# Turning an expert's gathered rows by transposing DMA transfers instead of on TensorE

## The chip, the cores and the metric

The kernel runs on one core of a Trainium2 chip. The metric is device time in microseconds. The kernel before takes 346.95 us, the median of three runs (346.88 to 347.78). The profile shown below is of one further execution under the hardware profiler, whose span is 321.0 us; positions in it ("at 159.71") are microseconds from the start of that span.

## The reference

A linear attention with a normalisation is followed by a layer of eight experts, of which each token uses one. Cut to what matters:

```python
# q, k, v: (8 batches, 8 heads, 576 tokens, 64)
kv  = einsum('bhsd,bhse->bhde', k, v)
out = einsum('bhsd,bhde->bhse', q, kv)
out = out / sqrt(mean(out * out, -1) + 1e-6) * g_norm
x   = out.transpose(0, 2, 1, 3).reshape(4608, 512)          # one row for each token

logits     = x @ w_gate                                     # (4608, 8)
expert_idx = argmax(logits, 1)
gate_w     = softmax(logits)[token, expert_idx]
for e in range(8):                                          # w1[e]: (512, 1024), w2[e]: (1024, 512)
    mask = expert_idx == e
    y[mask] = gate_w[mask] * (maximum(x[mask] @ w1[e], 0) @ w2[e])
```

## The kernel before

The attention stage computes the normalised rows in float16 and scatters each row, with its token number and its gate weight behind it, into a scratch in DRAM that has a region for each expert. The experts' stage works through nine jobs: experts 0 to 6, one tile of left-over rows, and expert 7. An expert's job gathers up to 640 rows, five tiles of 128 rows by 512 values. The first matrix product needs the rows turned, with the 512 values on the partitions. `flip` does that, a tile at a time:

```python
def flip(self, t):
    nt, xe = self.nt, self.xe
    if t == 0:
        self.xt = PF.tile([128, 4, nt * 128], F16, tag=f"xt{nt}", bufs=2, name="xt")
        self.idx = PF.tile([128, nt], I32, tag=f"idx{nt}", bufs=3, name="idx")
    xp = PSF.tile([128, 4, 128], F16, tag="xp", bufs=2, name="xp")        # PSUM
    for c in range(4):
        nc.tensor.transpose(xp[:, c, :], xe[t][:, c * 128:(c + 1) * 128], ident16)
    nc.vector.tensor_copy(self.xt[:, :, t * 128:(t + 1) * 128], xp)
    nc.vector.scalar_tensor_tensor(out=self.idx[:, t:t + 1], ...)         # rows of the output
```

The two products, `one` for a half of the columns and a block of 128 of the 1024 hidden values, `two` for a tile of rows:

```python
def one(self, ws, f):
    hp = PSF.tile([128, wd], F32, tag="hp", bufs=3, name="hp")            # wd = 320
    for kk in range(4):
        nc.tensor.matmul(hp, self.w.w1[:, kk, f * 128:(f + 1) * 128],
                         self.xt[:, kk, ws * wd:(ws + 1) * wd], start=(kk == 0), stop=(kk == 3))
    nc.scalar.activation(self.ht[:, f, ws * wd:(ws + 1) * wd], hp, ACTF.Relu)

def two(self, t):
    yp = PSF.tile([128, D], F32, tag="yp", bufs=3, name="yp")
    for f in range(8):
        nc.tensor.matmul(yp, self.ht[:, f, t * 128:(t + 1) * 128], self.w.w2[:, f, :],
                         start=(f == 0), stop=(f == 7))
    ys = PF.tile([128, D], F32, tag="ys", bufs=4, name="ys")
    nc.vector.tensor_scalar(ys, yp, self.xe[t][:, 514:516].bitcast(F32), None, op0=ALU.mult)
    nc.gpsimd.indirect_dma_start(out=self.views[t], ... in_=ys, ...)      # scatter to the output
```

The weights of an expert come in three steps: `stage` loads w1 in float32 into a single buffer `wst` from the queue of SyncE (SP), `scale` multiplies it by the norm's gain into a float16 buffer `w1e` (three buffers), and `second` loads w2 and casts it on the way, from the queue of GpSimd. Every engine works through its instructions in the order in which this code gives them:

```python
rows(0); W[1].second(); rows(1); W[2].second()       # rows(n): the five gathers of job n, on GpSimd
zp = PSF.tile([128, 512], F32, tag="yp", bufs=3, name="yp")
zeros(zp, 8)                                         # matmuls of zeros, to keep TensorE's clock up
for t in range(CT):                                  # CT = 5
    jobs[0].flip(t)
    zeros(zp, 2)

for n in range(len(order)):                          # nine jobs
    job = jobs[n]
    # ... n == 4: the left-over tile's gather, with its own row of the table
    nxt = jobs[n + 1] if n + 1 < len(order) else None
    rows(n + 2)
    flips = list(range(nxt.nt)) if nxt is not None else []
    for ws in range(job.halves):                     # two halves
        for f in range(8):
            job.one(ws, f)
            if ws == job.halves - 1 and f >= 2 and flips:
                nxt.flip(flips.pop(0))
            if ws == (n == 0) and f % 2 == 1 and n + 2 < len(order):
                W[n + 2].scale(nc.vector, f // 2)
                if f == 7 and n + 3 < len(order):
                    W[n + 3].stage()
    for t in range(job.nt):
        job.two(t)
    if n + 3 < len(order):
        W[n + 3].second()
```

Of the kernel before, what the change touches and what calls it, by code (L numbers as in the profile page):

```python
# [11 lines left out]
F32 = mybir.dt.float32  # L12
F16 = mybir.dt.float16
I32 = mybir.dt.int32
ALU = mybir.AluOpType
ACTF = mybir.ActivationFunctionType
AXX = mybir.AxisListType.X
# [4 lines left out]
def _bc(ap: bass.AP, insert_pos: int, count: int) -> bass.AP:  # L22
    dims = [list(d) for d in ap.ap]
    dims.insert(insert_pos, [0, count])
    return bass.AP(tensor=ap.tensor, offset=ap.offset, ap=dims)
# [3 lines left out]
def kernel(  # L29
# [11 lines left out]
    nc = tc.nc  # L41
# [3 lines left out]
    D = H * Dh  # L45
# [10 lines left out]
            name=f"I-{nc.next_id()}", act_func_set_id=ACT_SET_LN_EXP, ins=[], outs=[]  # L56
        )
    )

    xs = nc.dram_tensor("xs_scratch", (E * N, RW // 2), I32, kind="Internal")  # L60
    xs_views = dram_disjoint_views(xs.ap(), N // 128)
# [40 lines left out]
    ident16 = ch[:, 0:128]  # L102
# [10 lines left out]
    rowf = P_const.tile([128, E, CT], F32, tag="rowf")  # L113
    rowi = P_const.tile([128, E, CT], I32, tag="rowi")
    tabb = P_const.tile([128, 32], F32, tag="tabb")
# [6 lines left out]
    def zeros(t, n):  # L122

        for _ in range(n):
            nc.tensor.matmul(t, zero16, _bc(zero16, 1, 4), start=True, stop=True)
# [34 lines left out]
    with (  # L160
# [5 lines left out]
        for n in range(4):  # L166
            t = PA.tile([128, 4, 144], F32, tag=f"kvs{n}", name=f"kvs{n}")
# [252 lines left out]
        for b in range(1, B):  # L420
            f = first_slot[b]
# [137 lines left out]
    with (  # L559
# [14 lines left out]
        class Job:  # L574
# [8 lines left out]
            def flip(self, t):  # L583

                nt, xe = self.nt, self.xe
                if t == 0:
                    self.xt = PF.tile(
                        [128, 4, nt * 128], F16, tag=f"xt{nt}", bufs=2, name="xt"
                    )
                    self.idx = PF.tile([128, nt], I32, tag=f"idx{nt}", bufs=3, name="idx")  # L590
                xp = PSF.tile([128, 4, 128], F16, tag="xp", bufs=2, name="xp")
                for c in range(4):
                    nc.tensor.transpose(  # L593
                        xp[:, c, :], xe[t][:, c * 128:(c + 1) * 128], ident16
                    )
                nc.vector.tensor_copy(self.xt[:, :, t * 128:(t + 1) * 128], xp)  # L596

                nc.vector.scalar_tensor_tensor(
                    out=self.idx[:, t:t + 1], in0=xe[t][:, 512:514].bitcast(I32),
                    scalar=self.okm[:, t:t + 1], in1=self.bgm[:, t:t + 1],  # L600
                    op0=ALU.mult, op1=ALU.add,
                )
# [58 lines left out]
        with tc.manual_schedule(engines=by_hand):  # L661
            jobs = []
            for n, e in enumerate(order):
                if e == "left":
                    jobs.append(None)
                    continue
                jobs.append(Job(
                    [xe_bufs[(n % 3) * CT + t] for t in range(CT)], W[n],
                    valid[:, e, :], bigm[:, e, :], out_views[e * CT:(e + 1) * CT],
                ))  # L670

            def rows(n):
                if n < len(order) and order[n] != "left":
                    for t in range(CT):
                        gather(jobs[n].xe[t], rowi[:, order[n], t:t + 1])

            rows(0)
            W[1].second()
            rows(1)
            W[2].second()  # L680
            zp = PSF.tile([128, 512], F32, tag="yp", bufs=3, name="yp")
            zeros(zp, 8)
            for t in range(CT):
                jobs[0].flip(t)
                zeros(zp, 2)

            for n in range(len(order)):
                job = jobs[n]
                if n == 4:
                    jobs[7] = left_over(0, 3 * CT, out_views[E * CT])  # L690
                    W[7] = jobs[7].w
                nxt = jobs[n + 1] if n + 1 < len(order) else None
                rows(n + 2)
                flips = list(range(nxt.nt)) if nxt is not None else []
                for ws in range(job.halves):
                    for f in range(8):
                        job.one(ws, f)
                        if ws == job.halves - 1 and f >= 2 and flips:
                            nxt.flip(flips.pop(0))
                        if ws == (n == 0) and f % 2 == 1 and n + 2 < len(order):  # L700
                            W[n + 2].scale(nc.vector, f // 2)
                            if f == 7 and n + 3 < len(order):
# [6 lines that stand above are left out]
        nov = nc.values_load(tabi[0:1, 1, 7:8], min_val=0, max_val=NOV)  # L709
        with tc.If(nov > 1):  # L710
            with tc.For_i(1, nov) as t:
                job = left_over(t, 3 * CT, out_views[E * CT + 1])
# [36 lines left out]
```

## Time and profile before

| what | value |
|---|---|
| time, median of three | 346.95 us |
| span of the profiled execution | 321.0 us |
| TensorE busy | 276.2 us (86%) |
| VectorE busy | 161.1 us (50%) |
| ScalarE busy | 125.3 us (39%) |
| GpSimd busy | 160.8 us (50%) |
| transposes of gathered rows on TensorE (L593) | 164, mean 225 ns |
| copies of turned tiles on VectorE (L596) | 41, mean 419 ns |
| a w1 load (`wst`), from issue to landing | 12.7 us, median of 9 |
| a w2 load (`w2e`) | 13.6 us, median of 9 |
| a gather of a tile (`xe`) | 8.6 us, median of 40 |
| a scatter of a tile to the output | 3.9 us, median of 41 |

In the profile PE is TensorE, DVE VectorE, ACT ScalarE, POOL GpSimd and SP SyncE; PEld is the loading of TensorE's stationary operand, which overlaps its matmuls. A line in order of time has start, length, engine, source line, operation, what is written and what is read, shapes and how many; in brackets stands the idle time before it and what ended that. The lengths of matmuls overlap where they are pipelined, so what one costs is read from the starts. The DMA share is the mean busy share of the 16 DMA engines; it can go a little over 1, as it adds up packets that overlap. The clock is what TensorE was granted, 1.00 being full speed.

### The profile page before, as it was taken

How to read it: one execution, taken by the hardware profiler on the slowest of the kernel's cores; microseconds unless marked ns; L12 is line 12 of the kernel's file. 1: busy time of each engine (PE TensorE's matmuls, PEld its weight loads, DVE VectorE, ACT ScalarE, POOL GpSimd, SP SyncE). 2: the span in 40 equal slices, each digit the busy share in tenths (PEclk: the TensorE clock that was granted, in tenths of full speed). 3: DMA queues.
4: the chain of work that ended last, by engine and by line, in shares of the span. 5: the costliest groups of instructions: out<-in, count | busy, mean ns of one | idle time of the engine just before them, and what ended most of it. 6: DMA issues, size and time to landing. Idle time of an engine off the chain costs nothing.

```text
span 321.0 us, 6063 instructions
## 1 busy us (share of the span) xinstructions
PE 276.2 (86%) x2333; PEld 194.3 (61%) x2333; DVE 161.1 (50%) x415; ACT 125.3 (39%) x299; POOL 160.8 (50%) x188
## 2 busy tenths in 40 slices
PE   8769999899799397624699999999998999999990
PEld 3468978787687386511465655747465574747640
DVE  0023657857865637787426364636436273525040
ACT  1023654665465326452071532607153160713700
POOL 2095022283276626744787564836737444474041
PEclk9967999999999879857699999999999999999996
DMA  6999999999999994227699899695999969593021
GB/s 235 265 284 348 263 325 346 225 309 354 242 347 282 350 310 129 99 82 236 163 202 274 309 213 376 115 349 186 302 277 163 364 150 297 209 236 123 4 101 55
DMA packets 59726, 76.22 MB, mean 237 GB/s; under 512 B 16429, under 2 KB 50478, under 8 KB 59696
## 3 DMA queue, kind: packets, MB, share of 16 engines
q1 hardware_dynamic: 43360, 47.42, 48.6%
q0 software_dynamic: 16336, 28.40, 35.7%
q8 instruction: 19, 0.31, 0.4%
q14 instruction: 11, 0.09, 0.1%
HBM read 71.70 MB, written 15.50 MB: 272 GB/s over the span
## 4 chain that ended last, share of the span: by engine, by line
DMA 30%; PE 23%; issue 16%; POOL 12%; DVE 9%; SPq 3%; ACT 2%; POOLq 1%; DVEq 0%
DMA out_dram<-ys,idx 10%; PE op L294 7%; DMA xe<-xs_scratch,rowi 6%; DMA ld<-in_v_dram 6%; POOL out_dram L634 5%; DMA w2e<-in_moe_w_dram 5%; POOL xe L565 5%; PE kvp L232 4%; PE yp L626 3%; PE qtp L276 2%; PE kgp L254 2%; PE hp L612 2%; SPq L182 2%; DMA xs_scratch<-xg,sli 2%; DVE xg L327 2%
## 5 line engine op out<-in xcount | busy, mean ns | idle before, releaser
L619 ACT ACTIVATE ht<-hp 128x320 f16<-128x320 f32 (+1 forms) x136 | 58.1, 428 | 99.9 <-PE hp L612 90.8
L612 PE MATMUL hp<-xt,w1e 128*128 128x320 f16 (+1 forms) x544 | 78.7, 294 | 0.0
L626 PE MATMUL yp<-w2e,ht 128*128 128x512 f16 x328 | 72.3, 379 | 0.0
L634 POOL DMA_INDIRECT out_dram<-ys,idx x41 | 41.6, 1015 | 60.1 <-DVE ys L631 40.7
L631 DVE TENSOR_SCALAR ys<-yp,xe 128x512 f32<-128x512 f32 x41 | 30.8, 750 | 71.6 <-PE yp L626 49.0
L612 PEld LDWEIGHTS <-w1e 128*128 128x128 f16 x544 | 50.9, 98 | 18.6
L626 PEld LDWEIGHTS <-ht 128*128 128x128 f16 x328 | 32.1, 98 | 37.2
L404 POOL DMA_INDIRECT xs_scratch<-xg,sli x36 | 34.9, 970 | 30.6 <-DVE sli L400 20.1
L565 POOL DMA_INDIRECT xe<-xs_scratch,rowi x40 | 41.7, 1043 | 15.6 <-issue 11.6
L294 PE MATMUL op<-kvs,qts 128*128 128x144 f32 (+1 forms) x320 | 47.4, 309 | 1.7 <-ACT ex L376 0.7
L294 PEld LDWEIGHTS op<-kvs,qts 128*128 128x128 f32 (+1 forms) x320 | 39.7, 190 | 4.6 <-ACT sq L310 0.9
L213 POOL COPY qp<-ld 128x512 f32<-128x512 f32 x32 | 18.4, 615 | 45.1 <-DMA ld<-in_q_dram 45.1
L315 DVE TENSOR_REDUCE ms<-sq 128x8 f32<-128x512 f32 x36 | 24.5, 680 | 16.8 <-ACT sq L310 16.7
L310 ACT ACTIVATE sq<-op 128x512 f32<-128x512 f32 x36 | 21.4, 595 | 27.6 <-PE op L294 26.9
L281 ACT COPY qts<-qtp 128x512 f32<-128x512 f32 x36 | 20.9, 581 | 21.7 <-PE qtp L276 21.7
L232 PE MATMUL kvp<-ld 128*64 128x64 f32 x512 | 23.6, 239 | 4.8 <-DMA ld<-in_v_dram 4.8
L596 DVE COPY xt<-xp 128x512 f16<-128x512 f16 x41 | 17.2, 419 | 15.9 <-PE xp L593 15.6
L232 PEld LDWEIGHTS kvp<-ld 128*64 128x64 f32 x512 | 19.0, 147 | 9.4 <-issue 8.0
L327 DVE TENSOR_TENSOR xg<-op,rinv 128x512 f16<-128x512 f32 x36 | 24.5, 680 | 0.3
L593 PE MATMUL xp<-ch,xe 128*128 128x128 f16 x164 | 16.5, 225 | 8.8 <-DMA xe<-xs_scratch,rowi 7.4
L276 PE MATMUL qtp<-cf,qp 128*128 128x128 f32 x128 | 21.2, 293 | 1.7 <-POOL qp L213 1.7
L144 DVE TENSOR_SCALAR w1e<-wst,g 128x1024 f16<-128x1024 f32 x28 | 21.1, 804 | 1.8 <-DMA wst<-in_moe_w_dram 1.8
(93 smaller groups left out, 221.4 us busy)
## 6 DMA issues: line engine op xcount, KB each, us to landing
wst<-in_moe_w_dram SPq DMA_DIRECT2D x9, 2048.0 KB, 12.7
w2e<-in_moe_w_dram POOLq DMA_DIRECT2D x9, 1024.0 KB, 13.6
ld<-in_k_dram SPq DMA_DIRECT2D x8, 1024.0 KB, 10.8
ld<-in_v_dram SPq DMA_DIRECT2D x8, 1024.0 KB, 10.7
ld<-in_q_dram SPq DMA_DIRECT2D x8, 1024.0 KB, 9.0
kr<-in_k_dram SPq DMA_DIRECT2D x8, 128.0 KB, 9.9
vr<-in_v_dram SPq DMA_DIRECT2D x8, 128.0 KB, 7.1
qr<-in_q_dram SPq DMA_DIRECT2D x8, 128.0 KB, 6.7
```

The costliest lines, as they stand in the source:

```text
L232: nc.tensor.matmul(kvp[64 * hh:64 * hh + 64, i, :], lhs, rhs, start=(j == 0), stop=(j == 4),)
L276: nc.tensor.transpose(qtp[:, i, :], src[:, 2 * i:2 * i + 2, :], ident)
L294: nc.tensor.matmul(op[c, i // 2, c0:c0 + 144], qts[s][:, i, c], kvs[:, i, :], start=True, stop=True,)
L315: nc.vector.reduce_sum(ms, sq, axis=AXX)
L327: nc.vector.tensor_tensor(xg[:, r, 0:512].rearrange("p (c i h n) -> p c i h n", c=2, i=2, h=2), ox, _bc(r4, 4, 64), op=ALU.mult,)
L404: nc.gpsimd.indirect_dma_start(out=xs_views[9 * self.P + self.g0 + t], out_offset=IndirectOffsetOnAxis(ap=self.sli[:, t:t + 1], axis=0), i ...
L565: nc.gpsimd.indirect_dma_start(out=xe.bitcast(I32), out_offset=None, in_=xs.ap(), in_offset=IndirectOffsetOnAxis(ap=rows, axis=0), bounds_ ...
L612: nc.tensor.matmul(hp, self.w.w1[:, kk, f * 128:(f + 1) * 128], self.xt[:, kk, ws * wd:(ws + 1) * wd], start=(kk == 0), stop=(kk == 3),)
L619: nc.scalar.activation(self.ht[:, f, ws * wd:(ws + 1) * wd], hp, ACTF.Relu)
L626: nc.tensor.matmul(yp, self.ht[:, f, t * 128:(t + 1) * 128], self.w.w2[:, f, :], start=(f == 0), stop=(f == 7),)
L631: nc.vector.tensor_scalar(ys, yp, self.xe[t][:, 514:516].bitcast(F32), None, op0=ALU.mult)
L634: nc.gpsimd.indirect_dma_start(out=self.views[t], out_offset=IndirectOffsetOnAxis(ap=self.idx[:, t:t + 1], axis=0), in_=ys, in_offset=None ...
```

## The change

The transposes on TensorE, the PSUM tile and the copy go; in their place SyncE's queue issues one transposing DMA transfer for each gathered tile, from SBUF to SBUF. This takes work off TensorE and VectorE. `xt` gets a third buffer, since the transfers of the next job are asked for at the beginning of a job and no longer between its matmuls. The zero matmuls around the first job's transposes are replaced by 24 matmuls on a tile of zeros that VectorE clears after it has computed the first job's row numbers.

```diff
                     self.xt = PF.tile(
-                        [128, 4, nt * 128], F16, tag=f"xt{nt}", bufs=2, name="xt"
+                        [128, 4, nt * 128], F16, tag=f"xt{nt}", bufs=3, name="xt"
                     )
 ...
-                xp = PSF.tile([128, 4, 128], F16, tag="xp", bufs=2, name="xp")
-                for c in range(4):
-                    nc.tensor.transpose(
-                        xp[:, c, :], xe[t][:, c * 128:(c + 1) * 128], ident16
-                    )
-                nc.vector.tensor_copy(self.xt[:, :, t * 128:(t + 1) * 128], xp)
+                nc.sync.dma_start_transpose(
+                    out=self.xt[:, :, t * 128:(t + 1) * 128], in_=xe[t][:, 0:D]
+                )
 ...
             zp = PSF.tile([128, 512], F32, tag="yp", bufs=3, name="yp")
-            zeros(zp, 8)
             for t in range(CT):
                 jobs[0].flip(t)
-                zeros(zp, 2)
+            late0 = PF.tile([128, 128], F16, tag="late0", name="late0")
+            nc.vector.memset(late0, 0.0)
+            for _ in range(24):
+                nc.tensor.matmul(zp, late0, _bc(late0, 1, 4), start=True, stop=True)
 ...
                 rows(n + 2)
-                flips = list(range(nxt.nt)) if nxt is not None else []
+                for t in range(nxt.nt if nxt is not None else 0):
+                    nxt.flip(t)
                 for ws in range(job.halves):
                     for f in range(8):
                         job.one(ws, f)
-                        if ws == job.halves - 1 and f >= 2 and flips:
-                            nxt.flip(flips.pop(0))
```

More of the change, by code (lines that the diff above doesn't have):

```diff
@@ L14 @@
 I32 = mybir.dt.int32
+I16 = mybir.dt.int16
 ALU = mybir.AluOpType
```

## The prediction

> **What bounds the kernel now.** I read the page first for the slices, then the instructions in order of time on TensorE, then busy time by stretch, one stretch for each expert, and last the groups and the chain of waits. In the slices
>
> ```profile
> PE   8769999899799397624699999999998999999990
> PEclk9967999999999879857699999999999999999996
> DMA  6999999999999994227699899695999969593021
> ```
>
> the first half of the span is the attention stage, which the change doesn't touch. Slices 17 to 20 (some 136 to 160 us) are the hand-over: TensorE has little to do and its clock is down to 5 to 8 tenths. From slice 20 on come the experts, with TensorE at 9 tenths and full clock to the end. Each slice is 8.0 us. Is that 9 real work, or waiting that looks like work? The order of time on TensorE answers, here for the third expert:
>
> ```profile
> 197.56 6.14 PE L612 MATMUL hp<-xt,w1e 128*128 128x320 f16 x44
> 203.53 0.39 PE L593 MATMUL xp<-ch,xe 128*128 128x128 f16 x4
> 203.76 0.71 PE L612 MATMUL hp<-xt,w1e 128*128 128x320 f16 x4
> 204.30 0.39 PE L593 MATMUL xp<-ch,xe 128*128 128x128 f16 x4
> ...
> 206.82 0.71 PE L612 MATMUL hp<-xt,w1e 128*128 128x320 f16 x4
> 207.37 8.80 PE L626 MATMUL yp<-w2e,ht 128*128 128x512 f16 x40
> 216.00 6.14 PE L612 MATMUL hp<-xt,w1e 128*128 128x320 f16 x44
> ```
>
> No idle time is printed anywhere, so TensorE sets the pace. The step from start to start is the cost (the durations overlap): 44 hp take 203.53 - 197.56 = 5.97, or 0.136 us each; 40 yp take 8.63, or 0.216 each; four transposes take 203.76 - 203.53 = 0.23. An expert is 64 x 0.136 + 40 x 0.216 = 17.3 us of matmuls, plus five turned tiles at 0.23 = 1.13, which gives the measured 18.44.
>
> The stretches, one expert each, with PE, PEld, DVE, ACT, POOL busy time, then clock, DMA share and rate:
>
> ```profile
> 178.70:197.60 18.90, 18.61 (x126) 11.30 (x125) 9.20 (x19) 7.00 (x16) 11.13 (x12) 1.00 0.97 284
> 197.60:216.00 18.40, 18.40 (x126) 11.26 (x124) 9.52 (x19) 7.00 (x16) 9.82 (x10) 1.00 0.86 247
> 234.40:254.20 19.80, 18.69 (x126) 11.34 (x125) 9.63 (x22) 7.00 (x16) 11.14 (x11) 1.00 0.94 262
> 295.00:312.40 17.40, 17.40 (x105) 10.08 (x103) 3.75 (x5) 6.99 (x16) 4.51 (x5) 1.00 0.13 47
> ```
>
> The last expert, which has no next one to turn, takes 17.4. DMA is at 0.86 to 0.97 while weights flow: the second engine close to its limit, and the one that the change loads. In the attention stage, where TensorE does wait for loads, the same column stands at 1.10 with 306 GB/s (20 to 90 us), so I take 1.1 as full.
>
> The hand-over, TensorE and GpSimd in order of time:
>
> ```profile
> 144.58 3.42 PE L125 MATMUL yp<-zero 128*128 128x512 f16 x8 [0.26 <-DVE cnt L509]
> 155.04 0.61 PE L593 MATMUL xp<-ch,xe 128*128 128x128 f16 x4 [7.04 <-DMA xe<-xs_scratch,rowi]
> 155.44 1.06 PE L125 MATMUL yp<-zero 128*128 128x512 f16 x2
> ...
> 159.71 6.14 PE L612 MATMUL hp<-xt,w1e 128*128 128x320 f16 x44
> ```
>
> ```profile
> 150.28 1.05 POOL L565 DMA_INDIRECT xe<-xs_scratch,rowi  x1 [3.71 <-DVE cm L542]
> 155.56 1.00 POOL L565 DMA_INDIRECT xe<-xs_scratch,rowi  x1 [0.31 <-issue]
> ```
>
> The first gather of the first expert lands 4.7 us after its issue, at 155.0; the fifth, issued at 155.56, 2.7 later, at 158.3. The first real matmul starts at 159.71, 1.4 us after the last row is there. TensorE turns tiles and multiplies zeros from 155.04, and the granted clock is 0.50 from 152 to 157 and 1.00 from 158: it comes up after some 2.9 us of work.
>
> **What the Trainium skill says.** "Advanced Engine Details and Errata", section "X-Bar Transpose (TRN2)", holds transposing DMAs to be as fast as ordinary ones, 350 to 400 GB/s. "DMA: Bandwidth & Descriptors", section "Latency and other measured facts", has 261 GB/s where the middle dimension isn't contiguous, as in xt here. Neither is shown by the trace of before, which has no such transfer. The same page, section "Issuing engines are not separate DMA queues", says that all queues run on the same 16 engines; the trace agrees, in that a gather lands in 2.7 us in the quiet hand-over but in 12.9 us when issued at 223.46 behind w2e and beside wst. "TensorE: Matmul & The Clock Gate", section "Part 4: PE-mode transpose", gives about 275 ns for a transpose in a kernel; the mean recorded here is 225 ns, but back to back one costs only 0.23 / 4 = 57 ns of TensorE's time, and that is what removing it saves.
>
> **The change, part by part.**
>
> 1. Transposes off TensorE. Inside the experts' stage 36 tiles are turned (experts 1 to 7 have five each, the left-over tile one; those of expert 0 lie before it): 36 x 0.226 = -8.1 us, all on the path.
>
> 2. Copies off VectorE: 41 copies of 0.419 us are 17.2 us, no bound by themselves. But VectorE works in order, and where it waited for an output scatter (ys waiting for out_dram, 15.7 us in four waits) the copy came late and TensorE stopped. From 159.71 to 312.35 is 152.6 us; the matmuls need 8 x 17.3 + 3.5 for the left-over tile = 141.9, the transposes 8.1, so 2.6 us are such stops (the longest are 1.11, 0.34 and 0.29, with the matmuls around them stretched). The new feed of xt doesn't pass VectorE: -2.6.
>
> 3. The hand-over. SP now waits for each gather, transposes it, and TensorE waits. The W[2] load issued on SP at 146.38 lands in 8.3 us, at 154.7, so it isn't in the way. What is in the way is the block of 24 warming matmuls: they read late0, which VectorE clears only after the fifth idx, and that waits for the fifth gather at 158.3. Add some 0.4 for idx and memset: start at 158.7, with a cold clock, since the zeros between 144 and 159 are gone. At 0.43 us each (3.42 / 8) the first 2.9 us hold seven; the other 17 at 0.216 take 3.7. They end at 165.3. The three tiles that the first half needs have gathers landed by 156.0, and even at 2 us each would be turned by 163. So the first hp starts at about 165.4 instead of 159.71: +5.7.
>
> 4. Load on DMA. A tile is 128 x 512 x 2 bytes = 131 KB, at 261 GB/s 0.5 us of all engines, an estimate from the page above. Five per expert are 2.5 us. Now an expert's DMA work is about 0.9 x 18.5 = 16.7 in units of the share; with 2.5 it is 19.2, and at 1.1 it fits in 17.4 us, just as long as an expert will take (17.3). There is slack of most of an expert between a weight's landing and its use, and xt has three buffers, so a shortage comes out only in part. I put +2.6 for it, half a microsecond for each of the five experts during which weights still come.
>
> Sum: -8.1 - 2.6 + 5.7 + 2.6 = -2.4 us, 346.95 - 2.4 = 344.5. I carry the difference from the profiled span (321.0) to the unprofiled time one to one.
>
> **Rivals.** (a) The transposes are hidden and DMA has room: the term of 2.6 is nothing, and the time is 341.9. For it: each is asked for nearly an expert ahead, and only 0.13 of DMA is used in the last expert. Against: the 0.97 above. (b) DMA becomes the bound. The wst buffer is single: load (12.7 us median), four scalings on VectorE (3.0), next load, a loop of 15.7, and the transposes go through the same queue. Up to about 1.5 us for the five they fit into 17.3; at 2 us per tile the loop is 25.7, a drift of 8 per expert over five loops, less some 6 us before VectorE's wait reaches yp. That would make 360 to 375. For it: in the chain of waits DMA holds 30% and PE 23%, and GpSimd's round of w2e, five gathers and five scatters already takes 18.5 us (222.2 to 240.67), waiting 4.4 us for landings. Against: the skill's rates are four times better than 2 us. (c) The hand-over is worse than I have it, as expert 0's transposes take 3 us each beside the gathers of expert 1: first hp at 168 or later, 347 to 350. The writer's choice of 24 warming matmuls hints that they expected a wait of that length.
>
> **Range and chances.** The ideal, without any DMA shortage, is 341.9, so over 2% (below 340.0) needs the hand-over to be cheaper than the 24 matmuls allow: 0.07. Slower by over 2% (above 353.9) needs rival (b) in a mild form or (b) with (c): 0.2. Most lies between. The range has its tail on the slow side: 340.5 to 357.
>
> **What would show each step.** Step 1: start to start of 17.3 us for experts whose line shows no idle time. Step 2: no idle time before hp put down to VectorE. Step 3: 24 late0 matmuls from about 158.7 to 165.3, half of them at 0.43, and the first hp right behind; if hp waits for DMA xt after them, (c). Step 4: DMA share of 1.0 or more from 179 to 280, landings of wst over 12.7 and w2e over 13.6 us, and idle time before hp or yp that ends with a DMA. I am wrong if a transposing transfer takes well over 1 us of queue time: then wst lands after the point where VectorE wants it, and the experts' pitch rises above 18.4.

## The result and the profile after

The changed kernel takes 360.39 us, the median of four runs (360.05 to 368.66), against 347.0 us for the kernel before: ratio 1.0378, with a 95% interval of 1.0357 to 1.0398. It is slower by 13.4 us, where 2.4 us less was predicted, and lies outside the range of 340.5 to 357.

The first view is the slices of the changed kernel's page (9.0 us each, the span being 358.3), with its line for the hardware queues and the groups of the two products:

```profile
PE   8889998689858975220348999999998997978990
PEclk9959999969987997555586999999999898999997
DMA  7999999969997913116699889999999999999221
q1 hardware_dynamic: 65664, 52.80, 52.7%
L610 PE MATMUL hp<-xt,w1e 128*128 128x320 f16 (+1 forms) x544 | 75.9, 300 | 8.9 <-DMA xt<-xe 7.3
L624 PE MATMUL yp<-w2e,ht 128*128 128x512 f16 x328 | 76.5, 391 | 7.4 <-DVE ys L629 6.7
```

Beside the slices of before, three things are to be seen. The hole of the hand-over is longer. The DMA row, which had 5s, 6s and 7s among its 9s in the experts, is now a row of 9s with two 8s to near the end. And the two products, ahead of which TensorE never sat idle in the profile of before (both groups had 0.0), now wait: 8.9 us before `hp`, mostly for the turned tiles, and 7.4 before `yp`, mostly for VectorE's `ys`.

TensorE in order of time, from the end of the routing on (the brackets give the idle time ahead and what ended it):

```profile
161.25 0.19 PE L508 MATMUL cp<-cs,ch 128*128 128x8 f16 x1 [1.16 <-DVE cs L506]
176.17 7.41 PE L685 MATMUL yp<-late 128*128 128x512 f16 x24 [14.73 <-DVE late L683]
189.22 6.85 PE L610 MATMUL hp<-xt,w1e 128*128 128x320 f16 x32 [5.65 <-DMA xt<-xe]
196.64 4.51 PE L610 MATMUL hp<-xt,w1e 128*128 128x320 f16 x32 [0.57 <-ACT ht L617]
200.98 8.80 PE L624 MATMUL yp<-w2e,ht 128*128 128x512 f16 x40
209.62 8.86 PE L610 MATMUL hp<-xt,w1e 128*128 128x320 f16 x64
218.31 8.80 PE L624 MATMUL yp<-w2e,ht 128*128 128x512 f16 x40
226.94 5.33 PE L610 MATMUL hp<-xt,w1e 128*128 128x320 f16 x38
...
278.10 5.30 PE L624 MATMUL yp<-w2e,ht 128*128 128x512 f16 x16 [2.21 <-DVE ys L629]
299.98 5.22 PE L624 MATMUL yp<-w2e,ht 128*128 128x512 f16 x16 [2.38 <-DVE ys L629]
```

The 24 matmuls of zeros (`late`) end near 183.6, and then TensorE waits 5.65 us for the first turned tiles. The first `hp` comes 28.0 us after the routing's last matmul (189.22 - 161.25), where before it came 15.6 after (159.71 - 144.13). The second, third and fourth expert then take 17.3 us each from start to start (209.62 to 226.94 is the second), as step 1 has it. Later ones stop in the middle of `yp`.

The stretches of the hand-over, of the third expert and of two later ones (PE, PEld, DVE, ACT, POOL busy time, then clock, DMA share, GB/s):

```profile
176.00:189.00 13.00, 7.41 (x24) 2.73 (x24) 2.85 (x8) 0.00 (x0) 9.08 (x9) 0.76 1.17 187
226.90:244.30 17.40, 17.40 (x106) 10.21 (x105) 7.36 (x14) 7.00 (x16) 10.67 (x11) 1.00 1.11 230
261.60:283.20 21.60, 19.29 (x105) 10.60 (x104) 7.62 (x17) 6.79 (x16) 11.93 (x12) 0.92 1.08 245
283.20:305.00 21.80, 19.25 (x105) 10.53 (x104) 7.08 (x14) 6.82 (x16) 9.73 (x11) 0.92 1.10 235
```

DMA stands at 1.08 to 1.17, where the middle experts of before had 0.86 to 0.97, and moves fewer GB/s. In the last two lines TensorE is busy for 19.3 us with what takes 17.4 in the third expert, as the clock is at 0.92: behind the stops of 2.21 and 2.38 us its mean is 0.67 and 0.68 to the end of the expert. So these two experts are 4.3 and 4.5 us longer. Behind the stop of 2.13 us at 322.12 it stayed at 1.00. One of VectorE's waits in the experts names what `ys` waits for (us in all, times, longest):

```profile
DVE ys L629 <- DMA out_dram<-ys,idx: 48.2, 7, 13.7
```

It was 15.7 us in four waits before. The four `ys` buffers are full until a scatter to the output lands, and the scatters land late: the one that GpSimd issued at 261.73, behind a w2 load and five gathers, let VectorE go on at 272.42, 10.7 us later, where the slowest of before took 8.9.

**The sum, with both kernels measured in one sitting.** The kernel before took 318 to 322 us in some sittings on the chip and 344 to 348 in others, so times are compared only with the runs of before in the same sitting. The profile of before above and that of after come from sittings of different kinds. A pair of runs, `e15_before_pair` and `e16_after_pair`, has both in one (before there: 345.14 us, median of 19).

> The kernel before unchanged, to have its profile from the same chip as the changed kernel's in the next run. If the chip is one on which before takes about 345 us: routing's last matmul near 161, first hp 15.5 to 16 us later, and experts of about 160 us (155.5 of the run with eight ys buffers, plus the 4.8 by which that run was faster), with stops for ys. If the longer time of such chips lies in the attention stage alone, the experts take 152 to 154 us as on the others.

> The changed kernel unchanged, on the same chip as the run ahead. From routing's last matmul to the first hp 28 us against some 16 (+12). If before's experts take about 160 us on this chip, those of the changed kernel are equal to them within 2 us and the hand-over is the whole of a difference of 13 us; if they take 153, the experts lose 6 to 8 us and the kernel as a whole 20.

Measured: the changed kernel 360.25 us, ratio 1.0409 (1.0277 to 1.0541). First before, then after:

```profile
160.95 0.19 PE L507 MATMUL cp<-cs,ch 128*128 128x8 f16 x1 [1.15 <-DVE cs L505]
177.89 6.14 PE L612 MATMUL hp<-xt,w1e 128*128 128x320 f16 x44
...
325.66 8.80 PE L626 MATMUL yp<-w2e,ht 128*128 128x512 f16 x40
```

```profile
160.47 0.19 PE L508 MATMUL cp<-cs,ch 128*128 128x8 f16 x1 [1.16 <-DVE cs L506]
175.14 6.98 PE L685 MATMUL yp<-late 128*128 128x512 f16 x24 [14.48 <-DVE late L683]
188.72 10.51 PE L610 MATMUL hp<-xt,w1e 128*128 128x320 f16 x64 [6.61 <-DMA xt<-xe]
...
342.18 8.80 PE L624 MATMUL yp<-w2e,ht 128*128 128x512 f16 x40
```

The routing ends at the same place. From there to the first `hp` it is 16.9 against 28.3 us: +11.3. From the first `hp` to the end of the last `yp` it is 156.6 against 162.3: +5.7. With the 0.5 us by which the routing came earlier this makes 16.5, the whole difference of the spans (343.0 and 359.5). So neither expectation held alone: about two thirds are the hand-over, one third the experts (whose first job is 10.51 us in `hp` and not 8.86, as it begins with a low clock). From start to start, by job (the last of them to its end):

| job | 0 | 1 | 2 | 3 | 4 | 5 | 6 | left | 7 |
|---|---|---|---|---|---|---|---|---|---|
| before | 19.1 | 18.8 | 19.5 | 19.4 | 20.3 | 18.5 | 17.6 | 6.0 | 17.5 |
| after | 19.0 | 17.3 | 17.3 | 18.8 | 21.7 | 23.5 | 20.2 | 7.1 | 17.5 |

The jobs from the second to the fourth gain 4.3 us, and from the fifth on that is given back with interest.

### The profile page after: what moved, and what is told of

Same layout as the page of the kernel before. It is cut to its first block, busy times and chain, and to the rows that moved or that the text cites. A ratio compares the mean times of both kernels' runs of the same rounds, so it can differ in the third digit from the quotient of the medians.

```text
span 358.3 us, 5832 instructions
## 1 busy us (share of the span) xinstructions
PE 281.7 (79%) x2175; PEld 191.7 (53%) x2175; DVE 144.7 (40%) x375; ACT 125.1 (35%) x299; POOL 160.6 (45%) x188
## 2 busy tenths in 40 slices
DMA packets 82029, 81.57 MB, mean 228 GB/s; under 512 B 38733, under 2 KB 72782, under 8 KB 82000
## 4 chain that ended last, share of the span: by engine, by line
DMA 34%; PE 19%; issue 15%; DVE 12%; SPq 5%; POOL 4%; ACT 4%; another core or an unknown queue 3%; POOLq 1%; DVEq 0%
DMA out_dram<-ys,idx 9%; DMA xe<-xs_scratch,rowi 9%; DMA w2e<-in_moe_w_dram 7%; PE op L295 7%; DMA xt<-xe 7%; PE kvp L233 5%; POOL out_dram L632 3%; PE qtp L277 3%; DVE xg L328 2%; SPq L592 2%; PE kgp L255 2%; DVE ms L316 2%; SPq L183 2%; DMA g<-in_g_norm_dram 2%
## 5 line engine op out<-in xcount | busy, mean ns | idle before, releaser
L610 PE MATMUL hp<-xt,w1e 128*128 128x320 f16 (+1 forms) x544 | 75.9, 300 | 8.9 <-DMA xt<-xe 7.3
L624 PE MATMUL yp<-w2e,ht 128*128 128x512 f16 x328 | 76.5, 391 | 7.4 <-DVE ys L629 6.7
L610 PEld LDWEIGHTS <-w1e 128*128 128x128 f16 x544 | 52.7, 99 | 32.5 <-issue 10.6
L624 PEld LDWEIGHTS <-ht 128*128 128x128 f16 x328 | 32.9, 100 | 48.2 <-issue 13.0
L295 PE MATMUL op<-kvs,qts 128*128 128x144 f32 (+1 forms) x320 | 50.4, 325 | 9.1 <-DVE xg L328 8.6
L295 PEld LDWEIGHTS op<-kvs,qts 128*128 128x128 f32 (+1 forms) x320 | 42.5, 202 | 12.1 <-issue 9.4
L566 POOL DMA_INDIRECT xe<-xs_scratch,rowi x40 | 41.0, 1025 | 16.9 <-issue 11.6
L233 PE MATMUL kvp<-ld 128*64 128x64 f32 x512 | 26.2, 239 | 9.1 <-issue 8.9
L233 PEld LDWEIGHTS kvp<-ld 128*64 128x64 f32 x512 | 20.6, 146 | 13.5 <-issue 12.4
L685 PE MATMUL yp<-late 128*128 128x512 f16 x24 | 7.4, 480 | 14.7 <-DVE late L683 14.7
L324 DVE TENSOR_TENSOR lr<-op,rinv 128x64 f32<-128x64 f32 x36 | 8.1, 224 | 26.9 <-ACT rinv L322 17.8
```

The costliest lines, as they stand in the source:

```text
L233: nc.tensor.matmul(kvp[64 * hh:64 * hh + 64, i, :], lhs, rhs, start=(j == 0), stop=(j == 4),)
L295: nc.tensor.matmul(op[c, i // 2, c0:c0 + 144], qts[s][:, i, c], kvs[:, i, :], start=True, stop=True,)
L566: nc.gpsimd.indirect_dma_start(out=xe.bitcast(I32), out_offset=None, in_=xs.ap(), in_offset=IndirectOffsetOnAxis(ap=rows, axis=0), bounds_ ...
```

## The experiments

`A` is the changed kernel, `B` the one before. Each ratio is to `B` in the same sitting. No ratio is given where the runs of one kernel scatter too widely; their medians stand alone.

| run | what it is | us | B there | ratio (95%) |
|---|---|---|---|---|
| e0 | B again | 321.69 | 318.23 | 1.013 (1.002 to 1.024) |
| e1 | A, first expert on TensorE | 337.82 | 318.23 | none (329.94 to 342.5) |
| e2 | B, only the first expert by DMA | 334.4 | 318.23 | 1.051 (1.041 to 1.060) |
| e3 | A, nothing turned | 317.17 | 318.23 | 0.998 (0.994 to 1.001) |
| e4 | A again | 342.91 | 321.81 | none (336.8 to 345.43) |
| e5 | e2, DMA kept quiet meanwhile | 330.26 | 321.81 | 1.030 (1.019 to 1.042) |
| e6 | e1, w1 loads from another queue | 334.15 | 321.81 | 1.041 (1.032 to 1.049) |
| e7 | e1, weights of three experts only | 313.43 | 321.81 | 0.978 (0.966 to 0.989) |
| e8 | e1, no later tile turned | 340.94 | 345.14 | 0.987 (0.981 to 0.993) |
| e9 | B, eight ys buffers | 340.33 | 345.14 | 0.987 (0.982 to 0.992) |
| e10 | e6, eight ys buffers | 371.93 | 345.14 | none (363.67 to 373.52) |
| e11 | e8, eight ys buffers | 328.94 | 345.14 | 0.954 (0.949 to 0.958) |
| e12 | e1, w1 of three experts only | 336.01 | 347.81 | 0.966 (0.955 to 0.978) |
| e13 | e1, w2 of three experts only | 343.25 | 347.81 | 0.969 (0.963 to 0.975) |
| e14 | e1, eight ys buffers | 349.89 | 347.81 | 0.998 (0.994 to 1.001) |

Ratio and interval are worked out from the undisturbed runs, so a ratio isn't always the quotient of the two medians (in e13, where four of 18 runs count, 333.62 to 337.45 us, the quotient would be 0.987), and the profiled executions of e4 (345.43 us), e10 (373.01), e13 (341.86) and e14 (353.16) are not among those runs.

### The hand-over: e0 to e5

**e0**, the kernel before without an edit, as a measure for the first sitting.

> The kernel before, unchanged, profiled once more. Its profile on record has a span of 321.0 us although its median time is 346.95; in the profile of the changed kernel the attention stage, which both share, ends 17 us later (cp at 161.25 instead of 144.13). If that delay belongs to the kernel before as well, this span is about 345 and its attention stage ends at 155 to 165. If the change causes it, the span is 321 again and the attention stage ends at 144.

Routing to first `hp` is 15.9 us (142.88 to 158.75), the experts 153.8. That two runs of the same kernel come out at 1.013 (and 18 of them, e15, at 0.997) says how far a ratio from so few can be trusted. e5, e7, e12 and e16 have two runs as well.

**e2** is `B` with the change for the first expert alone, and **e1** its complement:

```diff
# e2, in flip of B                          (e1, in flip of A: the two branches exchanged)
+if self is jobs[0]:
+    nc.sync.dma_start_transpose(out=self.xt[:, :, t*128:(t+1)*128], in_=xe[t][:, 0:D])
+else:
     xp = ...; 4 x nc.tensor.transpose(...); nc.vector.tensor_copy(...)
# e2 also has A's 24 matmuls on late0 before the jobs; e1 has B's zeros(zp, 8) and zeros(zp, 2)
```

> The kernel before, but the first expert's five tiles are turned by DMA and followed by the 24 warming matmuls; all later tiles on TensorE. Theory A: +12 to +16 us on the kernel before, 359 to 363. Theory B: +3 to +6, 350 to 353.

> The changed kernel, but the first expert's five tiles are turned as before, on TensorE with zeros between; all later tiles by DMA. Theory A (most of the loss is the hand-over: first matmul 26.9 us after the row numbers instead of 14.5, and 3 us of cold clock): a gain of 12 to 16 us on the changed kernel, 344 to 348. Theory B (the loss is in the experts, from output scatters that land late behind the transfers): a gain of under 5, 355 to 360.

e2 shows the hand-over of the changed kernel and nothing else of it. TensorE and then SyncE's queue in order of time:

```profile
141.96 0.19 PE L507 MATMUL cp<-cs,ch 128*128 128x8 f16 x1 [1.18 <-DVE cs L505]
156.54 7.17 PE L692 MATMUL yp<-late 128*128 128x512 f16 x24 [14.39 <-DVE late L690]
169.68 6.57 PE L617 MATMUL hp<-xt,w1e 128*128 128x320 f16 x32 [5.97 <-DMA xt<-xe]
177.83 1.79 PE L617 MATMUL hp<-xt,w1e 128*128 128x320 f16 x12 [1.58 <-DMA xt<-xe]
```

```profile
154.17 9.88 SPq L592 DMA_TRANSPOSE xt<-xe  x5
```

The first `hp` comes 27.7 us after the routing, 11.8 later than in e0, and the kernel loses 5%. The third tile, which the first `hp` needs, was asked for at 157.0 and landed 12.5 us later. SyncE was held for 1.30, 1.44, 2.13, 3.24 and 1.58 us by the five transfers, so the queue is no long line; the transfers are slow to land. At that time GpSimd has w2 and the gathers of the next experts under way, and the DMA share is 1.06 to 1.50 (156 to 170).

**e3** leaves the turning out altogether (its output isn't the reference's): `xt` is one fixed tile, nothing is turned, and the 24 matmuls stay.

```diff
-self.xt = PF.tile([128, 4, nt * 128], F16, tag=f"xt{nt}", bufs=3, name="xt")
+self.xt = xt_fixed[:, :, 0:nt * 128]            # set to 0.03 once
-nc.sync.dma_start_transpose(...)
```

> The changed kernel without any turning: the first product reads one fixed tile, no transposing transfer is issued, so the output isn't the reference's. It shows what is left when the transfers cost nothing. Theory A: the first matmul follows the 24 warming ones at once; about 10 us less than the changed kernel before it even counts the experts, 340 to 346 in all if the late experts also recover. Theory B: the late experts fall from 21 to 22 us back to 17.3 to 18.5. If neither happens (355 or more) the transfers aren't the cause.

From routing to first `hp` it is 20.8 us (138.32 to 159.15): the 24 matmuls alone cost 20.8 - 15.9 = 4.9, and the landing the rest. The time is that of before, though neither TensorE nor DMA turns anything: the experts take 148.0 us against 153.8 in e0, and the 4.9 take most of that gain back. Nor do the experts come down to the prediction's 141.9 of pure matmuls: `yp` stops three times for `ys`, 5.1 us in all. Something else bounds them; e8 to e11 take that up.

**e4** is `A` unchanged, in one sitting with e5 to e7.

> The changed kernel unchanged, beside the others on one chip, where the kernel before takes 318 us. If the two losses found so far add up (first expert by DMA alone +16, all later tiles by DMA alone +20, but the first delay gives the transfers a head start), 335 to 345. In its recorded profile 197 us lie between the routing's last matmul and the end against 178 for the kernel before; if that carries over, 318 + 19 = 337.

Its hand-over is 28.7 us (141.20 to 169.91, with 7.4 of waiting for `xt`), some 13 more than before in e0. Its four runs spread from 336.8 to 345.43, 15 to 24 us above the 321.81 of `B`, so it isn't shown whether the change costs more here than the 13 to 15 us of the other sittings.

**e5** tells a slow transfer from a crowded one: e2, but GpSimd issues nothing more until it has read one column of each turned tile.

```diff
-rows(0); W[1].second(); rows(1); W[2].second()
+rows(0)
 for t in range(CT): jobs[0].flip(t)
+for t in range(CT):
+    nc.gpsimd.tensor_copy(seen[:, t:t+1], jobs[0].xt[:, 0, t*128:t*128+1])
+W[1].second(); rows(1); W[2].second()
```

> The kernel before with the first expert's tiles turned by DMA, as in the earlier run, but GpSimd issues the second weights and the gathers of experts 1 and 2 only when the five turned tiles have landed, and it reads one column of each tile as it lands, so the trace shows the landings. Theory C (a transposing transfer is cheap alone, and its 10 us and more come from the traffic beside it): landings 2 to 3 us after issue, about 1 us apart, and the first product no later than the 24 warming matmuls end; 323 to 328. Theory D (it is slow by itself): landings 5 us or more after issue or over 2 us apart, and no gain on the 334.4 of the run with traffic.

TensorE, and GpSimd's reads of the landed tiles:

```profile
156.27 6.68 PE L697 MATMUL yp<-late 128*128 128x512 f16 x24 [14.43 <-DVE late L695]
162.78 6.14 PE L617 MATMUL hp<-xt,w1e 128*128 128x320 f16 x44
```

```profile
159.11 0.19 POOL L688 COPY seen<-xt 128x1 f16<-128x1 f16 x1 [1.19 <-DMA xt<-xe]
160.38 0.19 POOL L688 COPY seen<-xt 128x1 f16<-128x1 f16 x1 [1.08 <-DMA xt<-xe]
161.69 0.19 POOL L688 COPY seen<-xt 128x1 f16<-128x1 f16 x1 [1.12 <-DMA xt<-xe]
```

Alone, a turned tile lands every 1.3 us, 2.5 us after its issue, and `hp` follows the matmuls of zeros without a wait. So the 12.5 us of e2 were the company of the gathers and weights. From 157 to 161 the DMA share is only 0.51, at 101 GB/s: the engines are half idle, while SyncE is held for 1.24 to 1.30 us by each transfer. The kernel still loses 3%. Some 5.3 us of it are the hand-over (21.1 us to the first `hp`, with the 24 matmuls, against 15.9), and gathers and weights now come late: the transposes of the second expert wait 2.36 and 0.71 us for its gathered rows.

### The experts, tiles that come late: e1, e6, e7, e12, e13

e1 has the hand-over of before (16.5 us), yet its experts take 164.4 us against 153.8 in e0. `hp` waits for `xt` six times, 17.5 us in all, and SyncE is held almost without a break:

```profile
172.25 18.30 SPq L600 DMA_TRANSPOSE xt<-xe  x5
190.66 0.53 SPq L135 DMA_DIRECT2D wst<-in_moe_w_dram  x1
191.28 19.82 SPq L600 DMA_TRANSPOSE xt<-xe  x5
211.21 0.55 SPq L135 DMA_DIRECT2D wst<-in_moe_w_dram  x1
```

Theory A, a gain of 12 to 16 us from the hand-over, isn't borne out: e1's runs lie 12 to 24 us above `B` in their sitting, those of the unmended kernel (e4) 15 to 24 in theirs. Five tiles take 18 to 20 us between two w1 loads, where five alone take 6.5. The hardware queues hold 58.9% of the 16 engines' span of 328.2 us, against 48.2% of 321.0 in e0: 38.6 us more for 36 tiles, 1.07 us of all engines for each. Two theories: the tiles are late because they share SyncE's queue with the w1 loads, or because the 16 engines are full.

**e6** moves the queue: w1 of the later experts is issued by ScalarE, behind its activations.

```diff
-W[n + 3].stage()                     # behind f == 7, from nc.sync
+W[n + 3].q = nc.scalar               # after the job's activations; "left" stays on nc.sync
+W[n + 3].stage()
```

> As the run with the first expert on TensorE and all later tiles by DMA (337.8), but the w1 loads of experts 3 to 6 and 7 are issued from ScalarE's queue, after the expert's activations, so that SyncE's queue holds the transfers alone. Theory E (the transfers wait because they stand behind a 2 MB load in one queue, and SyncE is held): the waits of the first product for xt go, 315 to 322. Theory F (the 16 DMA engines themselves are full): the order of queues changes little, 333 to 342.

The waits for `xt` in the middle are gone, but 3.72 and 7.19 us are left at the second and the last expert, and five stops for `ys` of 0.3 to 2.6 us have come. The time is hardly better: the wait moved to another transfer.

**e7** loads no weights after the first three experts; the later ones use those again (the output isn't the reference's).

```diff
-W[n + 3].stage()    -W[n + 2].scale(...) for n > 0    -W[n + 3].second()
+if n >= 3: job.w.w1, job.w.w2 = W[n % 3].w1, W[n % 3].w2
```

> As the run with the first expert on TensorE and all later tiles by DMA, but no weights are loaded after the first three experts; later experts reuse them, so the output isn't the reference's. The transfers, gathers and scatters stay. Theory F: with 4.2 MB less to read per expert no product waits for a turned tile, the experts follow each other at 17.3 us and the time is 309 to 314. If the experts still take 19 to 23 us, the transfers are slow for a reason of their own (330 or more).

The turning is as in e1, but from the third job on each expert takes 17.33 us, and one wait for `xt` (4.6 us, in the second) is all. So the transfers fit when weights don't compete. The run doesn't say whether by the queue or by the engines.

**e12** and **e13** do: each drops one half of these loads, 2.1 MB of reads for each later expert. Without w1, SyncE's queue is free for the turned tiles. Without w2, it is shared as before. (Outputs again not the reference's; without w1 VectorE's scaling goes too, without w2 one issue of GpSimd's for each expert.)

```diff
# e12: -W[n + 3].stage()  -W[n + 2].scale(...) for n > 0   +if n >= 3: job.w.w1 = W[n % 3].w1
# e13: -W[n + 3].second()                                  +if n >= 3: job.w.w2 = W[n % 3].w2
```

> The first expert is turned on TensorE, the later ones by DMA, and after the first three experts no w1 is loaded (the tiles in the buffers are used again), while w2 is loaded as before. This takes 2.1 MB of reads per expert away and leaves SyncE's queue to the turning transfers alone. If the late turned tiles come from sharing SyncE's queue with the w1 loads, and the next kernel (no w2) shows no such gain: about 0.98 to 0.99 of before, no hp that waits for xt behind the third expert, and a pitch of 17.3 to 19 us. If they come from DMA engines that are full: also about 0.98 to 1.00, but then the kernel without w2 gains as much.

> As the one ahead, but w1 is loaded and w2 is not: the same 2.1 MB of reads per expert are gone, and the turning transfers still stand between the w1 loads in SyncE's queue. If the shared queue is the cause: 1.02 to 1.05 of before, with hp still waiting 2 to 6 us per expert for xt. If full DMA engines are: about 0.98 to 1.00, the same as without w1, and waits for xt below 1 us behind the third expert.

Both gain, 0.966 and 0.969, more than was expected; but these are two runs and four of 18, and by the median of all its runs e13 has 0.987, so that they gain equally is not shown. The traces say more. TensorE's waits for the turned tiles, in e12 and then e13 (us in all, times, longest):

```profile
PE hp L618 <- DMA xt<-xe: 0.2, 1, 0.2
```

```profile
PE hp L618 <- DMA xt<-xe: 2.2, 1, 2.2
```

How long a transposing transfer held SyncE (ns: least, median, most) in e12, e13 and e14, which loads everything:

```profile
L600 SPq DMA_TRANSPOSE xt<-xe x36: 1191/1257/3966, 185.2 to 304.7; - x36
```

```profile
L600 SPq DMA_TRANSPOSE xt<-xe x36: 1188/1300/5721, 184.9 to 306.4; - x36
```

```profile
L600 SPq DMA_TRANSPOSE xt<-xe x36: 1191/2496/8537, 183.6 to 320.5; - x36
```

e1, with four `ys` buffers like e12 and e13, has a median of 2518 ns. With 2.1 MB less per expert the median hold falls to what one transfer takes alone, whichever queue the bytes had. So the shared queue is not what makes most tiles late; all the transfers together are too much. At most the single wait of 2.2 us in e13 may be the queue's.

### The experts, stops behind ys: e8 to e11 and e14

e3 had shown a second bound. **e8** is e1 with the later tiles not turned at all, which takes both the transposes and their transfers away (output not the reference's):

```diff
 if self is jobs[0]:
     ...                                          # on TensorE, as in e1
-else:
-    nc.sync.dma_start_transpose(...)             # later jobs read one fixed tile, as in e3
```

**e9, e10, e11** and **e14** are `B`, e6, e8 and e1 with one number changed:

```diff
-ys = PF.tile([128, D], F32, tag="ys", bufs=4, name="ys")
+ys = PF.tile([128, D], F32, tag="ys", bufs=8, name="ys")
```

> The first expert's tiles turned on TensorE as before; no later tile is turned at all (a fixed tile is read, so the output isn't the reference's). It is the most that this change could bring behind an undisturbed hand-over. If TensorE alone set the pace before, as the prediction has it, 36 transposes and the stops behind VectorE go: 10.7 us under the kernel before. Theory G (a second bound lies just below: GpSimd's round of one weight load, five gathers and five scatters, whose landings hold back ys and so yp): only 5 to 8 us under it, with waits of yp for ys of 1 to 2 us in experts 4 to 6.

> The kernel before with eight buffers for ys instead of four, so that VectorE doesn't wait for a scatter of the same expert to land. If the waits of ys for out_dram (15.7 us in four waits) are what makes xt late, the stops of TensorE go: 1 to 3 us under the kernel before. If the landings are late because DMA is full, nothing: within 1 us.

> All later tiles by DMA, w1 loads on ScalarE's queue, and eight buffers for ys: both ways in which the transfers were seen to hold up TensorE (xt late, ys held by scatters) are widened, only the load on DMA stays. If the losses came from queues and buffers, 310 to 318, under the kernel before. If the DMA engines are full (theory F), waits turn up somewhere else and it stays at 328 or more.

> As the first of these four (no later tile turned; output isn't the reference's) with eight buffers for ys. If theory G's second bound is only the number of ys buffers, the experts follow at 17.3 us and it lies 2 to 4 us under that run; if it is GpSimd's round itself, it is the same within 1 us.

> The change with its hand-over put back on TensorE (first expert) and eight ys buffers in place of four, all weights loaded as before. If the stops behind ys were what the experts lost and the DMA engines have room: 0.96 to 0.98 of before, with job pitches near 17.3 us. If the transfers of the turned tiles overfill the DMA engines: 1.02 to 1.05, with waits for xt or for weights in most experts.

e8 gains 1.3% only: its experts take 153.8 us, with three stops for `ys` of 3.9 us in all. It is 4.2 us under `B`, nearer to theory G's 5 to 8 than to 10.7. With eight buffers, e11, the stops are gone, and TensorE goes through all nine jobs without one printed idle time:

```profile
176.49 8.86 PE L617 MATMUL hp<-xt,w1e 128*128 128x320 f16 x64
185.19 8.80 PE L631 MATMUL yp<-w2e,ht 128*128 128x512 f16 x40
193.82 8.86 PE L617 MATMUL hp<-xtf,w1e 128*128 128x320 f16 x64
202.51 8.80 PE L631 MATMUL yp<-w2e,ht 128*128 128x512 f16 x40
...
310.14 8.80 PE L631 MATMUL yp<-w2e,ht 128*128 128x512 f16 x40
```

That is 142.4 us for the experts, close to the 141.9 of pure matmuls that the prediction worked out, and 4.6% off the whole. It takes both: no work of turning and room for scatters. The step from e8 to e11 is 12.0 us, where 2 to 4 were expected. Of the 11.4 in the experts' stage, the three experts with stops for `ys` account for 4.7; the other 6.7 lie in the left-over tile and the last expert, where e8's stops are put to ScalarE's `ht` or to nothing that the profile names. They are gone in e11 too, but why they were there isn't shown.

In e9 VectorE no longer waits for the output, and the kernel before is 4.8 us faster (1 to 3 were expected). By these ratios it is the fastest kernel of the study with the reference's output; but six runs and 1.3% are little beside the 1.013 and 0.997 of an unchanged kernel.

e14 is the change with its hand-over mended and its buffers added, the best that turning by DMA came to. It is as fast as before (0.998), so neither of its two forecasts held, and by the ratios slower than e9. The experts' stretch (whole stage, columns as above) in e11 and in e14:

```profile
176.50:318.90 142.40, 142.40 (x873) 83.94 (x871) 56.06 (x108) 57.74 (x136) 81.43 (x81) 1.00 0.86 238
```

```profile
179.00:343.00 164.00, 148.16 (x873) 84.70 (x871) 54.16 (x109) 56.92 (x136) 80.01 (x80) 0.98 1.03 235
```

The 36 transfers raise the DMA share from 0.86 to 1.03 over a stage that is longer, at the same GB/s, and TensorE stands still for 15.8 us of it. The longest two of TensorE's waits in this stage of e14:

```profile
PE hp L618 <- ACT ht L625: 6.2, 6, 1.8
PE hp L618 <- DMA xt<-xe: 6.1, 4, 2.4
```

Only the second is the turned tiles. In the first, ScalarE itself was waiting for `hp`, so the trace doesn't tell what held the two. e10 loses more than any other: a w1 load from ScalarE's queue took some 27 us from 196.3, VectorE waited 28.2 us for it, and TensorE 16.1. Its runs scatter, so only the kind of wait is taken from it: a bulk load suffers as the turned tiles do.

## Why the prediction was wrong

The prediction's sum has -8.1 - 2.6 + 2.6 = -8.1 us for the experts and +5.7 for the hand-over. The pair e15 and e16 has +5.7 and +11.3. So the larger part of the miss, 13.8 us, lies in the experts (steps 2 and 4; 1.7 of it is the low clock of the first job), and 5.6 in the hand-over (step 3).

**Step 1, the transposes, was right.** 17.3 us from start to start, for each expert that nothing stops: two in e16, three behind the first in the changed kernel's own profile, all in e11. The 8.1 us were gained and lost again.

**Step 2, the stops behind VectorE (-2.6), failed.** The stops were put down to the copy of the turned tile standing behind `ys` in VectorE's order. Removing the copy didn't remove what `ys` itself waits for: a free buffer, that is a landed scatter. With the scatters slower (10.7 us for the one above), `yp` met it directly, after its three PSUM buffers: VectorE's waits for the output rose from 15.7 to 48.2 us, and `yp` stopped for 6.7. e3 and e8 show such stops without any turning of later tiles, e11 shows them gone with eight buffers. One of the three stops that the prediction lists, the 0.34, was no stop behind VectorE either: the line at 166.19 of the profile of before says `[0.34 <-DMA xe<-xs_scratch,rowi]`, a wait for gathered rows. The number of buffers was in the code and the 15.7 us were in the prediction; what was missed is that they would outlive the copy.

**Step 3, the hand-over (+5.7), was right as far as its 24 matmuls go and mis-sized beyond.** They were to begin 14.6 us after the routing and began 14.9 after; alone they cost 4.9 (e3). The failing sentence is that the three tiles "even at 2 us each would be turned by 163", before the matmuls end. Alone that holds (e5: 1.3 us a tile). Beside the next experts' gathers and weights the third tile took 12.5 us to land (e2), so `hp` waited another 5.7 to 7.4 us: +11.3 in the pair of one sitting, +11.8 in e2. And TensorE, idle once more, began the first expert with a low clock (0.50 from 188.7 to 192 in e16): its first 64 `hp` took 10.51 us instead of 8.86. Rival (c) had this cause, with half the size or less (first `hp` at 168, 2.6 us behind the 165.4).

**Step 4, the load on DMA (+2.6), had the right cause and too small a size.** The mis-sized term is the 0.5 us of all engines for a tile, from the rate of 261 GB/s that the Trainium skill has in "DMA: Bandwidth & Descriptors", section "Latency and other measured facts". No run here shows that rate. Measured alone it is one tile in 1.3 us, 131 KB / 1.3 us = 101 GB/s, at a DMA share of 0.51, which makes 1.3 x 0.51 = 0.66 us of all engines (e5). In company each tile adds 1.07 us of all engines (e1 against e0), or 1.18 (e14 against e11: 54.9% of 351.4 less 45.9% of 327.5, by 36). These differences contain whatever the tiles lengthen of the other transfers in the same queues, so they are the price of turning a tile there and not its own time alone. By the same subtraction the hardware queues' time falls by 40.8 us without six w1 loads (e14 against e12), 6.8 each: turning five tiles of 0.66 MB weighs 5.3 to 5.9 us, nearly as much as loading 2.1 MB of weights. Put into the step's own sum, as an estimate, 16.7 + 5.3 = 22.0 over 1.1 is 20.0 us for an expert instead of 17.4, and the experts of e16 from the fourth to the seventh take 18.8 to 23.5. So it was DMA that set the pace, as step 4 feared and its number denied. That all queues run on the same engines (the same page, section "Issuing engines are not separate DMA queues") was cited, and e12 and e13 agree: a load gone from either queue brings the hold down to 1.3 us.

**The rivals.** (b), DMA as the bound, had the time (360 to 375) and the engine, but by another road: it wanted `wst` to come late through the shared queue, while in the changed kernel VectorE waits for `wst` once, 6.0 us, and the scatters and turned tiles are what come late. With the hand-over mended, `wst` does come late, as (b) has it: VectorE waits for it six times, 43.9 us in e1 and 57.5 in e14, against once and 1.8 us before; but no wait of TensorE there is put to weights. Its condition, 2 us a tile in the queue, is met in e1 and e14 by the median of 2.5 and isn't in the changed kernel's own profile (1.27), where the 12 us lost ahead of the experts give the early transfers time. Which wait takes the loss depends on such phases. (a), hidden transfers, fell.

**What stays open.** Why all kernels need some 17 to 20 us longer in some sittings up to the routing's end (138 to 144 us in some, 160 to 163 in others) is not known. It is so with and without the change (e9, e15), so no part of the result is put down to it. The loss in the experts isn't split between turned tiles, scatters and loads: moving one of them (e6, e10) brought out another, and 6.2 us of e14's stops name only ScalarE and TensorE. Nor do the runs tell apart whether the engines themselves are full or the memories behind them; the DMA share only says how long packets took.

## What to carry to other kernels

Before work is moved to the DMA engines, ask how full they are in that very stage, and count a transposing transfer by its time there, not its bytes: here 131 KB weighed like some 0.35 MB of a plain load. A transfer that is cheap alone is late in company, so a hand-over must not hang on one that starts beside the next stage's gathers and weights. And when one work of an engine that waits is removed, look at what it waited for: a ring of four buffers was the next bound. Doubling it went with 1.3% without any of the change, and with 3.5% where no later tile was turned (e8 to e11).

## What the hardware showed that was not expected

- A transposing transfer of a 128 x 512 tile of two-byte values within SBUF: issuing queue held for 1.24 to 1.30 us, landed 2.5 us after issue, one per 1.3 us in a row, at a DMA share of 0.51 (e5). Under load the queue was held for up to 8.5 us (e14).
- It is cut small: the changed kernel has 82029 DMA packets against 59726, 22303 more for 41 tiles, 544 each, or some 240 bytes a packet.
- A short stop of TensorE can cost twice: stops of 2.21 and 2.38 us lengthened an expert of the changed kernel by 4.3 and 4.5, with the granted clock at 0.92 over the stretch. But behind stops of 2.13 us in the same trace and of 2.41 and 2.55 us in e16 the clock stayed at 1.00; what decides isn't shown.
